# Weight conversion: the exact integer sum of exponent word and sign-and-rounding word is made by GpSimd instead of VectorE

## The chip, the cores and the metric

The kernel runs on one core of one Trainium2 chip. The metric is device time in microseconds; three runs of the kernel before took 594.98, 594.09 and 592.65 us, median 594.09 us. A core has TensorE (matmul), VectorE, ScalarE, GpSimd and SyncE, each with its own queue of instructions; in profiles they are PE (with PEld for weight loads), DVE, ACT, POOL and SP.

## The reference

A recurrent attention block (RWKV6) is followed by a two-layer network with an exact GELU:

```python
# r, k, v, w: (4, 8, 768, 48); u: (8, 48)
for t in range(S):
    kt, vt, rt, wt = (k[:, :, t], v[:, :, t], r[:, :, t], w[:, :, t])
    cur = np.einsum('bhd,bhe->bhde', u[None] * kt, vt)
    y[:, :, t] = np.einsum('bhd,bhde->bhe', rt, state + cur)
    state = wt[:, :, :, None] * state + np.einsum('bhd,bhe->bhde', kt, vt)

# x: y as (3072, 384); w_in: (384, 2048); w_out: (2048, 384), both float64
h = x @ w_in
g = 0.5 * h * (1.0 + erf(h * inv_sqrt2))
return (g @ w_out).astype(np.float32)
```

The two weight matrices come as float64 (a float32 array times a NumPy float64 scalar). The kernel takes them as 64-bit integers and makes float32 of them on the chip.

## The kernel before

The 3072 tokens are cut into eight blocks x of 384. For each block, `attention` (L373) makes the network's input xT, and `mlp` (L920) multiplies it by w_in, applies GELU and multiplies by w_out. While block x is attended to, the network of block x - 1 runs. The order in which instructions are issued is written out by hand: both are generators, and the strings in PLAN (L38) say, letter by letter, which generator does its next step. In block 0 the letters "." and "s" are the two halves of its attention, in block 1 "." is the network of block 0, "s" the attention of block 1 and "f" the beginning of the next block's; "l" loads, "w" makes masks and sums of w_out, "c" converts weights. Every engine works through its own queue in that order, and waits by semaphore for what it needs.

The weights are converted in blocks 0 and 1, in 16 pieces of 128x768 elements: eight of w_in, then eight of w_out. The steps of one piece, and their lines:

- A piece is loaded by SyncE into `raw`, of which there are five buffers (L212). Piece i + 3 is loaded once piece i is converted in program order, and takes over the buffer of piece i - 2.
- `prepare` (L342) runs on ScalarE: f is the high word's magnitude scaled by 2^-112 (L350), e is made of the low word in two steps, rounding it (L351, L352). f and e have two buffers each (HALFWAY), so piece i + 2 writes over those of piece i.
- `finish` (L355) runs on VectorE: f is shifted left by 3 (L363), e gets the sign of the high word (L365), and the result is the integer sum f + e, written into w_in_sb or w_out_sb (L369). The sum has to be exact in 32 bits; on VectorE it appears in the trace as one custom instruction over 128x1536 half-words.

`conversion` (L324) makes these into four steps of the letter "c": prepare the piece after this one, shift, sign, sum.

Around them in the queues of VectorE, ScalarE and TensorE in block 1 stand these lines, which the prediction speaks of: L472, the products of keys and receptances on TensorE, for six distances h; L525, the update of r and k on VectorE after each, and L536 and L485, which copy the products into a_sb under a mask (L533 does so on ScalarE for the last two distances); L514, the same updates as L525 in two single steps, in block 0; L705, transposes of k on TensorE, and L707, ScalarE's copy of them into kx; L731, products of kx and v; L746, the chain of states on VectorE; L772 and L817, the outputs of attention on TensorE, with a fence (L782, L784) between; L1074, the network's first product, with GELU on ScalarE (L1077, L1079); L1168, its second, which takes w_out_sb two rows of 128 per piece; L864, sums of w_out on VectorE. After block 1, L411, L398, L431 and L405 on VectorE begin the attention of block 2, whose first products are L608. GpSimd (iota, memset, an identity, and four copies at L306) has nothing to do after the first 20 us.

```python
            f = cv.tile([128, PIECE], U32, name="f")
            e = cv.tile([128, PIECE], U32, name="e")
            nc.scalar.activation(out=f.bitcast(F32), in_=hi.bitcast(F32), func=AF.Abs, scale=2.0 ** -112)
            nc.scalar.activation(out=e.bitcast(F32), in_=lo, func=AF.Identity, scale=2.0 ** -51, bias=two)
            nc.scalar.activation(out=e.bitcast(I32), in_=e.bitcast(F32), func=AF.Identity, scale=2.0 ** 22, bias=minus)
```

Of the kernel before, what the change touches and what calls it, by code (L numbers as in the profile page):

```python
# [11 lines left out]
U32 = mybir.dt.uint32  # L12
# [5 lines left out]
ALU = mybir.AluOpType  # L18
# [54 lines left out]
def kernel(  # L73
# [25 lines left out]
    nc = tc.nc  # L99
# [224 lines left out]
    def conversion():  # L324

        i = converted[0]
        if i >= len(pieces):
            return
        converted[0] += 1

        prepare(i + HALFWAY)
        yield
        if wide:
            yield from finish(pieces[i][0], raws[i], *halfway[i])
        for _ in weight_in(i + 3):
            pass
# [18 lines left out]
    def finish(dst, raw, f, e):  # L355

        hi = raw.bitcast(U32).rearrange("p (a b) -> p a b", b=2)[:, :, 1]

        nc.vector.tensor_scalar(out=f, in0=f, scalar1=3, scalar2=None, op0=ALU.logical_shift_left)  # L363
        yield
        nc.vector.scalar_tensor_tensor(out=e, in0=hi, scalar=0x80000000, in1=e,  # L365
                                       op0=ALU.bitwise_and, op1=ALU.bitwise_or)
        yield
        f, e = (z.rearrange("p (a c) -> p a c", a=dst.shape[1]) for z in (f, e))
        nc.vector.tensor_tensor(out=dst.bitcast(U32), in0=f, in1=e, op=ALU.add)  # L369

    xT_of = {}

# [955 lines left out]
```

## Time and profile before

| | |
|---|---|
| median of three runs | 594.09 us (592.65 to 594.98) |
| span of the profiled execution, first to last instruction | 591.6 us |
| TensorE busy (matmul) | 573.7 us, 97% |
| VectorE busy | 453.5 us, 77% |
| ScalarE busy | 279.8 us, 47% |
| GpSimd busy | 8.0 us, 1%, 21 instructions |
| granted TensorE clock | 1.00 throughout |

The page gives the profiled execution's span only; the three times beside it are of other executions. How busy each engine is in the stretches of blocks 0 and 1, in us (number of instructions):

```
core 0: us, PE busy (x) PEld busy (x) DVE busy (x) ACT busy (x) POOL busy (x), PEclk, DMA share, GB/s
30.00:45.00 15.00, 11.81 (x480) 10.20 (x483) 12.58 (x42) 9.80 (x20) 0.00 (x0) 1.00 0.59 190
45.00:60.00 15.00, 14.95 (x230) 9.40 (x229) 14.71 (x22) 11.77 (x24) 0.00 (x0) 1.00 0.86 302
60.00:75.00 15.00, 15.00 (x163) 9.10 (x163) 14.90 (x18) 12.84 (x24) 0.00 (x0) 1.00 0.54 168
75.00:90.00 15.00, 15.00 (x218) 9.73 (x211) 12.92 (x17) 12.86 (x22) 0.00 (x0) 1.00 0.76 274
90.00:105.00 15.00, 15.00 (x248) 9.91 (x250) 14.19 (x30) 13.07 (x18) 0.00 (x0) 1.00 0.17 55
105.00:120.00 15.00, 15.00 (x244) 11.85 (x237) 14.59 (x25) 4.49 (x10) 0.00 (x0) 1.00 0.12 37
```

A busy share says how much an engine had to do, not whether anything waited for it. That is read from the chain of work that ended last, from the waits, and from the order of the instructions in time. An instruction's line in the order of time gives its start, its length, the engine, the line, the operation, output and inputs, and in brackets the idle time before it and what ended it.

### The profile page before, as it was taken

The page shows a single profiled execution, that of the slowest core. Times are in us where ns is not written, and L with a number is a line of the kernel's source. Part 1 is how long each engine was busy: PE and PEld are TensorE (multiplying, and loading weights), DVE is VectorE, ACT ScalarE, POOL GpSimd, SP SyncE. Part 2 cuts the span into 40 slices and gives each one's busy share as a digit, 9 for nine tenths or more (in the row PEclk, how much of TensorE's full clock was granted, in tenths as well). Part 3 has the DMA queues.
Part 4 walks back from the last instruction along what each step waited for, and adds up shares of the span by engine and source line. Part 5 has one row for each costly group of instructions (what it writes and reads, how often), then busy time and mean ns, then how long its engine had stood idle before and what let it go on. Part 6 is the DMA issues. An engine that isn't in the chain of part 4 may idle for free.

```text
span 591.6 us, 17422 instructions
## 1 busy us (share of the span) xinstructions
PE 573.7 (97%) x7522; PEld 510.8 (86%) x7536; DVE 453.5 (77%) x871; ACT 279.8 (47%) x648; POOL 8.0 (1%) x21
## 2 busy tenths in 40 slices
PE   5779999999999999999999999999999999999998
PEld 3566666766799999999999999999999999999997
DVE  5989989998969986787859987688859998421432
ACT  2367889223612558046462458145560465435400
POOL 3100000000000000000000000000000000000000
DMA  6658581020142302241032311330025200210000
GB/s 237 197 192 308 163 287 56 32 89 2 29 140 78 108 22 35 76 125 38 1 61 84 122 38 21 93 120 2 2 34 160 72 2 8 35 46 0 1 14 33
DMA packets 51004, 46.80 MB, mean 79 GB/s; under 512 B 31728, under 2 KB 36080, under 8 KB 50928
## 3 DMA queue, kind: packets, MB, share of 16 engines
q1 hardware_dynamic: 50832, 45.62, 25.6%
q8 instruction: 59, 0.97, 0.7%
q14 instruction: 17, 0.14, 0.1%
q10 hardware_dynamic: 96, 0.07, 0.1%
HBM read 36.24 MB, written 4.72 MB: 69 GB/s over the span
## 4 chain that ended last, share of the span: by engine, by line
PE 91%; DVE 3%; DMA 2%; issue 1%; ACT 1%; SPq 0%; DVEq 0%; ACTq 0%
PE o_ps L1088 33%; PE h_ps L949 16%; PE u_ps L949 14%; PE h_ps L1074 11%; PE d L608 4%; PE o_ps L1168 4%; PE d L472 2%; PE y_ps L772 2%; PE y_ps L817 2%; PE kv_ps L731 2%; DVE st L746 1%; DMA rkw<-in_rkw_dram 1%; DMA raw<-in_w_in_dram 1%; ACT a_sb L533 1%; PE d L599 1%
## 5 line engine op out<-in xcount | busy, mean ns | idle before, releaser
L949 PE MATMUL h_ps<-xT,w_in_sb 128*128 128x192 f32 x480 | 95.5, 330 | 0.4 <-DVE o_sb L1185 0.4
L949 PEld LDWEIGHTS h_ps<-xT,w_in_sb 128*128 128x128 f32 x480 | 79.7, 190 | 4.0 <-ACT g L981 1.5
L1074 PE MATMUL h_ps<-xT,w_in_sb 128*128 128x384 f32 x192 | 64.2, 490 | 0.1
L1074 PEld LDWEIGHTS h_ps<-xT,w_in_sb 128*128 128x128 f32 x192 | 35.8, 190 | 24.1 <-ACT xT L824 0.4
L1088 PE MATMUL o_ps<-w_out_sb,g 128*128 128x192 f32 x224 | 39.7, 326 | 0.0
L1088 PEld LDWEIGHTS o_ps<-w_out_sb,g 128*128 128x128 f32 x224 | 37.0, 190 | 0.3
L949 PE MATMUL u_ps<-s,w_in_sb 128*128 128x192 f32 x192 | 35.3, 327 | 0.0
L624 ACT COPY a_sb<-d 32x256 f32<-32x256 f32 (+8 forms) x90 | 32.6, 363 | 4.6 <-PE d L608 3.1
L472 PEld LDWEIGHTS d<-rkw 64*64 64x64 f32 x1152 | 19.5, 138 | 15.6 <-issue 10.0
L949 PEld LDWEIGHTS u_ps<-s,w_in_sb 128*128 128x128 f32 x192 | 31.7, 190 | 0.2
L1088 PE MATMUL o_ps<-w_out_sb,f 128*128 128x192 f32 x176 | 31.6, 329 | 0.0
L1088 PE MATMUL o_ps<-t,g 128*128 128x192 f32 x176 | 31.4, 329 | 0.0
L1088 PE MATMUL o_ps<-w_out_sb,e 128*128 128x192 f32 x176 | 31.4, 329 | 0.0
L1088 PE MATMUL o_ps<-t,e 128*128 128x192 f32 x176 | 31.2, 328 | 0.0
L1088 PE MATMUL o_ps<-t,s 128*128 128x192 f32 x176 | 30.9, 327 | 0.0
L746 DVE SCALAR_TENSOR_TENSOR st<-st,tot_sb,kv_ps 128x48 f32<-128x48 f32 x160 | 29.0, 258 | 1.7 <-PE kv_ps L731 1.6
L472 PE MATMUL d<-rkw 64*64 64x64 f32 (+1 forms) x1152 | 22.1, 225 | 8.1 <-DMA rkw<-in_rkw_dram 4.1
L641 DVE COPY_PREDICATED a_sb<-quarter,d 128x480 f32<-128x480 uint8 (+5 forms) x54 | 23.2, 438 | 8.6 <-PE d L608 7.3
L1088 PEld LDWEIGHTS o_ps<-t,g 128*128 128x128 f32 x176 | 28.7, 190 | 0.4
L1088 PEld LDWEIGHTS o_ps<-w_out_sb,e 128*128 128x128 f32 x176 | 28.7, 190 | 0.3
L1088 PEld LDWEIGHTS o_ps<-w_out_sb,f 128*128 128x128 f32 x176 | 28.7, 190 | 0.3
L1088 PEld LDWEIGHTS o_ps<-t,e 128*128 128x128 f32 x176 | 28.8, 190 | 0.2
(165 smaller groups left out, 1134.0 us busy)
## 6 DMA issues: line engine op xcount, KB each, us to landing
rkw<-in_rkw_dram SPq DMA_DIRECT2D x54, 256.0 KB, 3.8
raw<-in_w_out_dram SPq DMA_DIRECT2D x8, 768.0 KB, 4.4
v_in<-in_v_dram SPq DMA_DIRECT2D x8, 584.0 KB, 3.9
raw<-in_w_in_dram SPq DMA_DIRECT2D x5, 768.0 KB, 7.0
out_dram<-o_sb SPq DMA_DIRECT2D x20, 192.0 KB, 2.0
rkw<-kx SPq DMA_DIRECT2D x72, 48.0 KB, 2.1
rkw<-in_rkw_dram SPq DMA_DIRECT2D x6, 384.0 KB, 5.5
raw<-in_w_in_dram SPq DMA_DIRECT2D x9, 256.0 KB, 5.1
```

The lines of the kernel that those rows point to most:

```text
L472: nc.tensor.matmul(d[half[p], g, n * width:(n + 1) * width], lhsT=kc[half[g], b, i, p], rhs=right(half[g], b, i, p), start=True, stop=True)
L608: nc.tensor.matmul(o[half[p], i * 3 * C // 2:(i + 1) * 3 * C // 2], lhsT=kc[half[g], n // NI, n % NI, p], rhs=rx[half[g], 2 * n + p], star ...
L624: nc.scalar.copy(out=at[z, g, first:behind, (a + 1) * h:], in_=d[z, :, :, to] if g == slice(None) else d[z, :, to])
L641: nc.vector.copy_predicated(out=an[:, :, :, :, (a + 1) * h:], mask=mask.to_broadcast(data.shape), data=data)
L731: nc.tensor.matmul(kv_ps[half[g], p, i * D:(i + 1) * D], lhsT=k_t(b, i, p, g), rhs=vs(b, i, g)[half[p], 0:D], start=True, stop=True)
L746: nc.vector.scalar_tensor_tensor(out=stq[:, q, c], in0=stq[:, q, c - 1] if c else b4[:, q, NC - 1], scalar=totq[:, q, c:c + 1], in1=kvs[q ...
L772: nc.tensor.matmul(y[p][half[g ^ swap(b)], i * C:(i + 1) * C], lhsT=vs(b, i, g)[half[p]], rhs=at[half[p], g, b * NI + i, :], start=(i == 0 ...
L817: nc.tensor.matmul(ys[b][0][c % 2][half[g ^ swap(b)], i * C:(i + 1) * C], lhsT=src[half[g], o:o + G], rhs=rc[half[g], b, i, c % 2], start= ...
L949: nc.tensor.matmul(o, lhsT=lhsT, rhs=rhs, start=start, stop=True, skip_group_check=True)
L1074: nc.tensor.matmul(h_ps, lhsT=w_in_sb[:, f // FI, j, f % FI * 128:(f % FI + 1) * 128], rhs=xT[:, j, :], start=(j == 0), stop=(j == NJ - 1))
L1088: nc.tensor.matmul(o, lhsT=lhs(j), rhs=rhs(j), start=start and j == 0, stop=(j == HF - 1), skip_group_check=True)
L1168: nc.tensor.matmul(o, lhsT=block(i, f // HF, f % HF), rhs=w_out_sb[:, f, :], start=(f == 0), stop=(f == NF - 1))
```

## The change

The sum at L369 is issued on GpSimd's queue. Operands, output and operation are as before; on GpSimd the addition of 32-bit words is an instruction of its own, over 128x768 words. The order of the steps stays, and so do the buffers.

```diff
@@ -366,7 +366,7 @@
                                        op0=ALU.bitwise_and, op1=ALU.bitwise_or)
         yield
         f, e = (z.rearrange("p (a c) -> p a c", a=dst.shape[1]) for z in (f, e))
-        nc.vector.tensor_tensor(out=dst.bitcast(U32), in0=f, in1=e, op=ALU.add)
+        nc.gpsimd.tensor_tensor(out=dst.bitcast(U32), in0=f, in1=e, op=ALU.add)
 
     xT_of = {}
 
```

## The prediction

> **What bounds it now.** I read the chain that ended last first, over the whole span and then from the start to 180 us; then the instructions that touch the tile f; then the two queues around the conversion, in order of time; then what little GpSimd does.
>
> ```profile
> PE 91%; DVE 3%; DMA 2%; issue 1%; ACT 1%; SPq 0%; DVEq 0%; ACTq 0%
> ```
>
> ```profile
> 84.16 1.53 PE d L472 x96
> 85.69 7.94 PE o_ps L1168 x24
> 93.62 1.53 PE d L472 x96
> 95.16 2.78 PE o_ps L1168 x8
> 97.93 1.31 PE kt_ps L705 x12
> 99.24 1.29 PE o_ps L1168 x4
> 100.54 1.54 PE kv_ps L731 x96
> ```
>
> The columns are start, length and work. From 45 us on, the chain is TensorE's own list with no gap. VectorE's time is worth nothing there unless TensorE comes to wait for it; lateness of VectorE, ScalarE or the weights costs as soon as it uses up its slack.
>
> ```profile
> L369 DVE CUSTOM_DVE_ANT_0 w_in_sb<-f,e x8: 941/954/958, 31.8 to 73.1; 128x1536 uint16<-128x1536 uint16 x8
> L369 DVE CUSTOM_DVE_ANT_0 w_out_sb<-f,e x8: 953/958/960, 75.4 to 106.8; 128x1536 uint16<-128x1536 uint16 x8
> ...
>   ACT f L350: 0.6, 1
> ```
>
> These are the sixteen additions, 0.95 us each, 31.8 to 107.8 us. The last line is the only wait that an addition ends: ScalarE, once, 0.6 us, for a buffer of f. TensorE never waited for one.
>
> **The change, part by part.** *Removed:* 16 additions from VectorE's queue. From one start to the next instruction's they hold 0.87 us (97.89 to 98.76), so 14 us in all. Does that shorten anything? On TensorE between 25 and 122 us, waits ended by VectorE are 1.0 (L525), 0.7 (fence) and 0.5 us (L363) on the weight loads, all before 43 us, where only addition 0 has gone before. The gain on the chain is therefore 0, at most about 1 us.
>
> *Added:* 16 additions of 128x768 words on GpSimd. No two-input GpSimd instruction is in this trace. The nearest rows:
>
> ```profile
> L271 POOL MEMSET a_sb<- 128x1536 f32 x1 | 1.4, 1378 | 2.2 <-DVE a_sb L270 2.2
> L301 POOL MEMSET rkw<- 128x512 f32 x1 | 0.5, 525 | 8.4 <-DVE rkw L514 8.4
> ...
> L306 POOL COPY rkw<-ident x4: 403/412/1134, 17.0 to 18.4; 32x128 f32<-32x128 f32 x4
> ```
>
> The two memsets give (1378 - 525) / 1024 = 0.83 ns per element and 0.10 us fixed. One addition reads two words per element: at twice the memset's rate 0.10 + 768 x 1.67 ns = 1.38 us, the lower end. The copy of 128 elements takes 412 ns undisturbed: (412 - 98) / 128 = 2.45 ns per element, so 0.10 + 768 x 2.45 ns = 1.98 us, and 3.86 us if a second input doubles it, the upper end. I take 2.0 us: the copy is the only row that reads and writes, and its scattered writes make up for its missing input.
>
> *The wait it brings.* The same copies show what GpSimd and VectorE do to each other:
>
> ```profile
> 17.30 1.03 DVE L485 COPY_PREDICATED a_sb<-mask,d 128x768 f32<-128x768 uint8 x1
> 18.25 0.95 DVE L525 TENSOR_TENSOR rkw<-rkw,tot_sb 128x768 f32<-128x768 f32 x1
> ```
>
> ```profile
> 18.35 1.13 POOL L306 COPY rkw<-ident 32x128 f32<-32x128 f32 x1
> ```
>
> Three copies beside L485, which has one operand in SBUF (the mask) and one in PSUM, took 0.40 to 0.41 us. The fourth began 0.10 us into L525, which reads two SBUF tensors, and took 1.13 us: it ended at 19.48, 0.28 us after L525. So GpSimd waited for a two-read VectorE instruction. The reverse, VectorE held by GpSimd, isn't shown; I price it at the whole rest of the addition, with 0 as the other end. What stands behind an addition in VectorE's queue is mostly of this kind: L363 (0.55 us for 768 words, against 0.95 us for L365, so at about twice the rate; taken as blocked), L365 and L525 (two reads); only L536, L485 and L746 are free.
>
> The Trainium skill, page "SBUF — State Buffer", section "Who interferes with whom", says that GpSimd shares one port pair with VectorE as an exclusive lock for a whole instruction, against VectorE instructions with two SBUF inputs or in a two-port mode: the loser waits it out. The copy's 1.13 us agrees for GpSimd as loser; by the page VectorE loses as much, and without it the sum below would be 0. The page "GPSIMD Engine Reference", section 3.1, measures a 2048-element addition at 4497 ns there and 2293 ns on VectorE; its estimate for 768 would be 1.69 us, and the sum about +3 us.
>
> *The walk.* I lay the queue out again with 2.0 us per addition, each starting when L365 is done and the port is free, and later instructions kept in program order. An addition with a two-read instruction behind it costs VectorE 2.0 in place of 0.87: +1.1 us. One that lies under COPY_PREDICATED gives back 0.87. L365 of pieces 3 to 12 then stands at +0.2, -0.7, +0.5, +1.6, +1.9, +3.0, +3.2, +2.4, +3.2, +4.3 us; two VectorE waits for ScalarE (0.44 and 1.31 us near 82 us) take up what piece 10 gives back. TensorE's bursts L472 don't notice: L525 ends 3.5 to 6 us ahead of each. At 95 us it is otherwise:
>
> ```profile
> 93.53 0.95 DVE L864 TENSOR_TENSOR t<-w_out_sb 128x768 f32<-128x768 f32 x1
> 95.22 1.76 DVE L525 TENSOR_TENSOR rkw<-rkw,tot_sb 128x1536 f32<-128x1536 f32 x1 [0.74 <-PE d L472]
> 96.90 0.95 DVE L365 SCALAR_TENSOR_TENSOR e<-raw,e 128x768 uint32<-128x768 uint32 x1
> ```
>
> ```profile
> 94.68 0.89 ACT L350 ACTIVATE f<-raw 128x768 f32<-128x768 f32 x1
> ...
> 97.46 1.59 ACT L533 COPY a_sb<-d 32x768 f32<-32x768 f32 x2
> 99.08 1.50 ACT L707 COPY kx<-kt_ps 128x768 f32<-128x768 f32 x2
> ```
>
> L525 ends at 96.98 and the transposes L705 that read its k start at 97.77: slack 0.8 us. The walk has L525 at 99.85 to 101.6 (addition 11 until 94.2, L365 of piece 12, L864, addition 12 until 98.5, L363, L864, L525). L705 is 3.8 us late. On ScalarE, L350 of piece 14 waits for addition 12 because both use one of two buffers of f, and queued behind it are L533 and L707, whose kx the matmuls L731 read; L707 would end at 104.45 instead of 100.58, no later than L731 needs with TensorE 3.8 us late. Next, L365 of piece 15 comes behind L746 and its addition ends at 115.75; TensorE's rows 14 of L1168, at 110.5 before, stand at 114.3: another 1.4 us. The stage after adds 0 to 0.4 us (VectorE's next deadline, L608 at 136.06, has 1.5 us). Together 5.5 us.
>
> That has GpSimd take the port as soon as it falls free. If VectorE's next two-read instruction always takes it first, additions run only in VectorE's gaps: addition 11 begins at 92.1, 12 at 94.1, L525 ends at 99.2 (L705 +1.5), L731 waits for kx (+2.0), and the last addition ends at 113.4 to 116.3, for 2.9 to 5.8 us in all. The trace doesn't say which; I take 4.5 us, between them. The earlier stretch costs nothing: additions 0 and 1, startable at 30.5 and 34.6 us, are wanted first by L350 at 39.1 and 48.7; the L514s behind them may be 1 to 2 us late, against the fence at 41.7 us at most +1.2 (taken as 0, kept for the range). No DMA moves: the raw buffers come free with L365, not with the addition, and GpSimd's queue is empty after 19.5 us.
>
> *Sum:* span 591.6 + 4.5 = 596.1. The three runs lie 1.1 to 3.4 us above that span, their median 2.5: 598.6 us.
>
> **Rivals.** *Hidden (not slower).* VectorE isn't held by a GpSimd read, or the addition is near 1.38 us. For it: the slack at every L472, 2.3 us or more from each addition's end to its weights' first matmul (least for addition 3, 58.8 to 61.1); ScalarE's one wait (for addition 3 behind L525, L536 and L485) goes too. Against: the 1.13 us copy. Two-read and double-rate work on VectorE from 45 to 107 us is L365 14 x 0.87, L363 14 x 0.47, L525 6 x 1.7, L431 2.7 and L864 3 x 0.87, together 34; 62 - 34 leaves 28 us for 14 additions, 2.0 each if all were packed perfectly. Well under that, at 1.4 us, it decides: +0 to 1, 594.1 to 595.
>
> *A slow addition.* At 3.86 us the port needs 34 + 14 x 3.86 = 88 us where 62 are there; about 6 us of slack go off: +20, 614 us. At 2.7 us it would be some +10, 604. It decides from 2.4 us on. Against it: the memset's 0.83 ns.
>
> *Faster.* VectorE's relief would have to remove TensorE waits; the three that it ends come to 2.2 us on the weight loads, so 592 us at best, and 3 us of gain has no place to come from.
>
> **Numbers.** What a measurement here can tell from no change is 0.5%, 3.0 us, so slower is above 597.1 and faster below 591.1. Forecast 0.55, with its own range 596 to 601, of which a fifth lies below 597.1; slow addition 0.14; hidden 0.27; faster 0.04. Slower 0.44 + 0.14 = 0.58, same 0.11 + 0.27 = 0.38, faster 0.04. The range takes in most of hidden and the milder half of slow: 593.8 to 607.
>
> **What would show it.** Right: sixteen GpSimd additions near 2 us (longer where they wait); L363, L365 or L525 longer than 0.55, 0.95 and 1.75 us, or gaps before them; TensorE waiting for L525 at L705, for L707 at L731 and for the last addition at L1168; ScalarE's L350 waiting for GpSimd. Wrong: VectorE's rows unchanged beside GpSimd's reads, additions under 1.5 us, or TensorE without a gap from 95 to 116 us.

## The result, and the profile after

Seventeen runs of each: 598.04 us after (595.07 to 599.67), 593.50 us before (592.24 to 597.27). The ratio is 1.0060, 95% interval 1.0045 to 1.0075: 3.6 us slower, between 2.7 and 4.5. (The two medians alone are 4.5 us apart, at the upper end of that interval; the ratio is made from all the runs.) The forecast was 598.6 us in a range of 593.8 to 607, with 0.58 on "slower by over 0.5%". The profiled execution's span is 597.5 us, against 591.6.

The groups of instructions that touch f, kernel after: count, then shortest, median and longest in ns, then when the first and the last began; under them, who waited for these.

```profile
L363 DVE TENSOR_SCALAR f<-f x16: 544/556/2174, 27.7 to 106.5; 128x768 uint32<-128x768 uint32 x16
L369 POOL TENSOR_TENSOR w_in_sb<-f,e x8: 1804/2314/3332, 30.1 to 77.3; 128x768 uint32<-128x768 uint32 x8
L369 POOL TENSOR_TENSOR w_out_sb<-f,e x8: 1818/2277/3268, 80.3 to 113.1; 128x768 uint32<-128x768 uint32 x8
...
  ACT f L350: 1.5, 3
  PEld kt_ps L705: 1.0, 1
```

ScalarE waits three times for a buffer of f, 1.5 us in all. The last line is a weight load of TensorE at 33 us, in block 0. L705 reads no sum there: it reads k, and the L514 that updates k stood 2.17 us instead of 0.55 beside addition 0 (30.77 to 32.94 us), so that TensorE's matmuls of L705 began only at 33.09, after a wait of 0.56 us.

An addition takes 1.80 us on GpSimd when nothing disturbs it (0.95 on VectorE), and up to 3.3 us when something does. What does is seen in the order of time, kernel after, VectorE first:

```profile
63.06 1.76 DVE L525 TENSOR_TENSOR rkw<-rkw,tot_sb 128x1536 f32<-128x1536 f32 x1
64.74 2.17 DVE L363 TENSOR_SCALAR f<-f 128x768 uint32<-128x768 uint32 x1
66.83 1.87 DVE L536 COPY_PREDICATED a_sb<-mask,d 128x768 f32<-128x768 uint8 x1
```

```profile
63.17 3.32 POOL L369 TENSOR_TENSOR w_in_sb<-f,e 128x768 uint32<-128x768 uint32 x1 [3.57 <-DVE e L365]
```

The addition is released at 63.17, 0.11 us into L525, and ends at 66.49: it waited until L525's end at 64.82 and then needed 1.67 us. L363, next in VectorE's queue, begins at 64.74 on paper and ends at 66.91: 2.17 us where 0.55 is its length, so it stood for 1.62 us. So the two exclude each other, and here the one that waits gets the next turn. A whole hold like this one costs VectorE 1.62 us, and the removed addition gives back 0.87.

What TensorE made of it, kernel after, between 97 and 113 us:

```profile
97.34 1.60 PE L472 MATMUL d<-rkw 64*64 64x32 f32 x96
98.87 2.85 PE L1168 MATMUL o_ps<-w_out_sb,g 128*128 128x384 f32 x8
101.90 1.53 PE L705 MATMUL kt_ps<-ident,rkw 128*128 128x128 f32 x12 [0.18 <-DVE rkw L525]
103.27 1.46 PE L1168 MATMUL o_ps<-w_out_sb,g 128*128 128x384 f32 x4
104.65 1.61 PE L731 MATMUL kv_ps<-v_in,kx 64*64 64x48 f32 x96
106.20 2.85 PE L1168 MATMUL o_ps<-w_out_sb,g 128*128 128x384 f32 x8
108.97 0.93 PE L772 MATMUL y_ps<-a_sb,v_in 64*64 64x64 f32 x48
111.93 0.93 PE L772 MATMUL y_ps<-a_sb,v_in 64*64 64x64 f32 x48 [2.03 <-DVE st L746]
```

In the kernel before this stretch had no gap. Its end there, with the chain of states L746 on VectorE first:

```profile
102.31 3.58 DVE L746 SCALAR_TENSOR_TENSOR st<-st,tot_sb,kv_ps 128x48 f32<-128x48 f32 x20
```

```profile
100.47 1.61 PE L731 MATMUL kv_ps<-v_in,kx 64*64 64x48 f32 x96
102.01 2.85 PE L1168 MATMUL o_ps<-w_out_sb,g 128*128 128x384 f32 x8
104.79 1.82 PE L772 MATMUL y_ps<-a_sb,v_in 64*64 64x64 f32 x96
106.54 6.72 PE L1168 MATMUL o_ps<-w_out_sb,g 128*128 128x384 f32 x20
```

In the kernel after, TensorE waits 0.2 us for L525 at L705 and 2.03 us for L746 in the middle of L772: its second half writes a pair of PSUM banks that L746 still reads (three such pairs take turns in the kernel, and the second y_ps gets the pair of the first kv_ps). And the whole stretch is late already when it begins: L472 starts at 97.34, not at 93.55. That 3.8 us arose before 53.5 us, where L1074's first long run starts (49.67 before). So the profile has two places, and the experiments had to price them apart.

### The profile page after: what moved, and what is told of

It is laid out like the page before. It is cut to its first block, busy times and chain, and to the rows that moved or that the text cites. A ratio compares the mean times of both kernels' runs of the same rounds, so it can differ in the third digit from the quotient of the medians.

```text
span 597.5 us, 17440 instructions
## 1 busy us (share of the span) xinstructions
PE 577.2 (97%) x7536; PEld 512.0 (86%) x7536; DVE 456.8 (76%) x855; ACT 280.0 (47%) x648; POOL 46.2 (8%) x37
## 5 line engine op out<-in xcount | busy, mean ns | idle before, releaser
L1074 PE MATMUL h_ps<-xT,w_in_sb 128*128 128x384 f32 x192 | 64.4, 491 | 2.9 <-DMA xT<-ysb 2.0
L1074 PEld LDWEIGHTS h_ps<-xT,w_in_sb 128*128 128x128 f32 x192 | 35.7, 190 | 27.4 <-issue 3.9
L472 PEld LDWEIGHTS d<-rkw 64*64 64x64 f32 x1152 | 19.6, 138 | 14.8 <-issue 10.6
L746 DVE SCALAR_TENSOR_TENSOR st<-st,tot_sb,kv_ps 128x48 f32<-128x48 f32 x160 | 29.0, 257 | 1.7 <-PE kv_ps L731 1.6
L1088 PEld LDWEIGHTS o_ps<-t,s 128*128 128x128 f32 x176 | 28.8, 190 | 0.1
```

The source lines that it names most:

```text
L472: nc.tensor.matmul(d[half[p], g, n * width:(n + 1) * width], lhsT=kc[half[g], b, i, p], rhs=right(half[g], b, i, p), start=True, stop=True)
L746: nc.vector.scalar_tensor_tensor(out=stq[:, q, c], in0=stq[:, q, c - 1] if c else b4[:, q, NC - 1], scalar=totq[:, q, c:c + 1], in1=kvs[q ...
L1074: nc.tensor.matmul(h_ps, lhsT=w_in_sb[:, f // FI, j, f % FI * 128:(f % FI + 1) * 128], rhs=xT[:, j, :], start=(j == 0), stop=(j == NJ - 1))
L1088: nc.tensor.matmul(o, lhsT=lhs(j), rhs=rhs(j), start=start and j == 0, stop=(j == HF - 1), skip_group_check=True)
```

## The experiments

Each was timed in five rounds against the kernel before on the same chip. A kernel that chooses the engine by piece has one more line, so its numbers behind L369 are one higher (L746 is L747 there).

**The changed kernel again.**

> The changed kernel once more, for a second profile of it. Two theories of its 4.5 us. Port: VectorE's two-read and double-rate instructions are held while GpSimd's additions read, the lateness grows from 50 us on, and TensorE pays from 98 to 113 us (L705, L772, L1168). Early: additions 0 and 1 hold L514, TensorE stands still near 38 us, the clock falls, the transfers of xT land late, and TensorE's first long run of L1074 begins late; what follows is covered by that. Port expects that run's start to vary between the profiles (49.7 us in the kernel before, 53.5 in the first profile of this one) while L1168's last rows stay 4 to 6 us late; early expects the run to begin 3 to 4 us late again. Both: 4 to 5 us above the kernel before.

596.82 us against 593.53; ratio 1.0061 (1.0040 to 1.0082). L1074's long run began at 52.74 us, L1168's last rows at 112.05 (106.54 before). The two late waits came back (0.16 us at L705, 2.03 at L772). The run was 3.1 us late again, as "early" had expected, but not all of that comes from additions. ScalarE's L350 of piece 1 waits for that piece's weights to land; it began at 29.02 us, against 27.70 before, and the granted clock was 0.50 between 30 and 32 us, while the first addition began at 32.60. From L350 of piece 1 to the long run it was 21.97 us in the kernel before, 26.78 in the first profile of the change, 23.72 in this one. So this profile alone doesn't decide between the two theories.

**Which additions cost.** The edit, with another set of pieces each time:

```diff
-        nc.gpsimd.tensor_tensor(out=dst.bitcast(U32), in0=f, in1=e, op=ALU.add)
+        engine = nc.gpsimd if converted[0] <= 2 else nc.vector
+        engine.tensor_tensor(out=dst.bitcast(U32), in0=f, in1=e, op=ALU.add)
```

> Only the additions of pieces 0 and 1 are on GpSimd, the other fourteen on VectorE as before. Early: 2.5 to 4 us slower than before, with TensorE idle for 2 us near 38 us and a granted clock under 0.8 after it. Port: L514 is held for 1 to 2 us, but VectorE's lateness is taken up before 50 us; 0 to 1 us slower.

> Additions 0 and 1 are on VectorE as before, the other fourteen on GpSimd. Port: 3 to 5 us slower than before, with TensorE waiting at L705 or L772 between 98 and 112 us. Early: at most 2.5 us slower, since the first stall is gone and with it most of the cost.

> Only the eight additions of w_out (pieces 8 to 15) are on GpSimd. Port: VectorE has 6 us of slack up to piece 10 and 0.8 us at L525 before L705; five additions before it are on GpSimd at some 0.9 us of lateness each, less the waits of 0.4, 1.3 and 0.7 us that VectorE has there: 2 to 4 us slower than before. Early: no more than 1 us slower.

| additions on GpSimd | ratio (95%) | us over 593.53 | L350 of piece 1 to the long run | wait at L772 |
|---|---|---|---|---|
| 0 and 1 | 1.0022 (1.0001 to 1.0043) | +1.3 | 22.41 us | none |
| 2 to 15 | 1.0061 (1.0037 to 1.0085) | +3.6 | 22.13 us | 2.03 us |
| 8 to 15 | 1.0044 (1.0025 to 1.0063) | +2.6 | 22.17 us | 2.02 us |
| all (again) | 1.0061 (1.0040 to 1.0082) | +3.6 | 23.72 us | 2.03 us |

(Microseconds are the ratio less one, times 593.53.) The early theory falls as the main cause: without additions 0 and 1 the cost is all there, and alone they cost 1.3 us with 0.1 to 2.6 in the interval, more than the 0 to 1 of "port" and less than the 2.5 to 4 of "early". The two parts, 1.3 and 3.6, sum to 4.9 where all sixteen cost 3.6; the intervals (2.4 to 4.9 for all, 2.2 to 5.0 for 2 to 15) allow it, so the share of additions 0 and 1 is known only roughly. "Port" holds in part. It priced 8 to 15 rightly, but said that lateness grows from 50 us on, and then 2 to 7 should add to it. The wait at L772 is the same 2.0 us with and without them. So the next pair asked where VectorE's lateness begins to count.

> Additions 2 to 9 are on GpSimd, the other eight on VectorE. Catching up: VectorE's lateness from these is gone when it waits for TensorE at L525 after the product of distance 16 (near 86 us), so TensorE has no new wait at L705 or L772: within 1 us of the kernel before. Running total: the lateness grows from 50 us on and reaches L705: 2 us or more slower.

> Only additions 13 and 14 are on GpSimd. Catching up: they hold L365 of piece 14 and L363 of piece 15 for 1.6 us each and save 0.87 us each, so L746 is 1.5 us late; TensorE's second half of L772 needs the bank that L746 reads and has 0.1 to 0.2 us of slack, so a wait of 1.3 us at L772 and none at L705; 1 to 2 us slower. Weights: if the last additions' own lateness were what counts, no wait at L772 and less than 0.5 us.

Additions 2 to 9: 593.37 us against 593.58, ratio 0.9998 (0.9979 to 1.0016), nothing. Their holds are there (an addition takes 2.7 us in the mean for w_in, L363 0.82 us instead of 0.55), yet TensorE has no wait at L705 or L772. VectorE's queue in that run shows why:

```profile
80.67 1.81 DVE L363 TENSOR_SCALAR f<-f 128x768 uint32<-128x768 uint32 x1 [0.51 <-ACT f L350]
82.53 0.96 DVE L365 SCALAR_TENSOR_TENSOR e<-raw,e 128x768 uint32<-128x768 uint32 x1
...
84.72 1.76 DVE L526 TENSOR_TENSOR rkw<-rkw,tot_sb 128x1536 f32<-128x1536 f32 x1 [0.23 <-PE d L473]
```

The same place in the kernel before:

```profile
83.58 0.96 DVE L365 SCALAR_TENSOR_TENSOR e<-raw,e 128x768 uint32<-128x768 uint32 x1 [1.31 <-ACT e L352]
...
85.75 1.76 DVE L525 TENSOR_TENSOR rkw<-rkw,tot_sb 128x1536 f32<-128x1536 f32 x1 [0.23 <-PE d L472]
```

L363 is held for 1.26 us. That goes into the 1.31 us that VectorE used to wait for ScalarE before L365, and then VectorE waits for TensorE, 0.23 us as in the kernel before. The product of distance 16 (L472, L473 here) and the L525 behind it are 1.67 us apart in both kernels (84.08 to 85.75 before, 87.87 to 89.54 after): whatever was late on VectorE has been caught up there.

Additions 13 and 14 alone: 594.66 us, ratio 1.0019 (1.0001 to 1.0037), 1.1 us. VectorE and then TensorE:

```profile
99.11 2.57 DVE L365 SCALAR_TENSOR_TENSOR e<-raw,e 128x768 uint32<-128x768 uint32 x1
101.61 0.95 DVE L865 TENSOR_TENSOR t<-w_out_sb 128x768 f32<-128x768 f32 x1
102.48 2.18 DVE L363 TENSOR_SCALAR f<-f 128x768 uint32<-128x768 uint32 x1
104.58 3.57 DVE L747 SCALAR_TENSOR_TENSOR st<-st,tot_sb,kv_ps 128x48 f32<-128x48 f32 x20
```

```profile
101.34 1.61 PE L732 MATMUL kv_ps<-v_in,kx 64*64 64x48 f32 x96
102.88 2.85 PE L1169 MATMUL o_ps<-w_out_sb,g 128*128 128x384 f32 x8
105.66 0.93 PE L773 MATMUL y_ps<-a_sb,v_in 64*64 64x64 f32 x48
107.95 0.93 PE L773 MATMUL y_ps<-a_sb,v_in 64*64 64x64 f32 x48 [1.36 <-DVE st L747]
```

Two holds of 1.6 us, less two additions of 0.87: the chain of states begins 3.24 us after L731's first matmul, against 1.84 us before (100.47 to 102.31), so 1.40 us late, and TensorE waits 1.36 us. With all of 10 to 14 on GpSimd it begins 3.90 us after (104.65 to 108.55), 2.06 us late, and TensorE waits 2.03 us. The slack at this place is under 0.05 us. "Weights" is out: nothing waits for a sum itself in this profile. Additions 10 to 12 were not run alone.

**Is it the reading?** Both kernels keep every sum on VectorE and give GpSimd something beside it that nobody uses:

```diff
+        beside = s_home[:, 0:PIECE].bitcast(U32)
+        nc.vector.memset(beside[:, 0:1], 0)
+        nc.gpsimd.tensor_tensor(out=beside, in0=beside, in1=beside, op=ALU.add)   # beside_read
+        for _ in range(2):                                                        # beside_write
+            nc.gpsimd.memset(beside, 0)
         nc.vector.tensor_tensor(out=dst.bitcast(U32), in0=f, in1=e, op=ALU.add)
```

(One or the other; s_home is cleared once at its making.)

> The kernel before, with every sum on VectorE; beside each, GpSimd adds 128x768 words of a scratch tile to themselves into the same tile (released by a one-word VectorE memset after L365), and nothing reads it. Port: VectorE's two-read and double-rate instructions are held for up to 1.7 us beside each, sixteen times, with nothing saved for it: L369 or L363 or L525 stretched, 4 to 12 us slower. Rival (the cost comes from the sum's result or the buffers being late, for ScalarE and TensorE): within 1 us of the kernel before.

> As the run beside_read, but GpSimd only writes the scratch tile: two memsets of 128x768 words, 0.74 us each, in the place of its addition. If the hold is by GpSimd's reading: L365, L369 and L525 keep 0.95, 0.95 and 1.75 us, at most L363 is longer, 0 to 1.5 us slower. If any GpSimd instruction on this memory holds VectorE: 3 to 10 us slower, and L525 or L369 stretched by 0.7 us and more.

The reading neighbour: 608.12 us, ratio 1.0232 (1.0207 to 1.0258), 13.8 us slower, more than the theory's 4 to 12. The writing one: 593.94 us, 0.9998 (0.9983 to 1.0014), nothing. VectorE's groups between 25 and 125 us, first beside reads, then beside writes (L364 and L366 are L363 and L365; L529 and L530 are L525):

```profile
L364 DVE TENSOR_SCALAR f<-f 128x768 uint32<-128x768 uint32 x16 | 18.0, 1123 | 0.0
L529 DVE TENSOR_TENSOR rkw<-rkw,tot_sb 128x1536 f32<-128x1536 f32 x5 | 12.6, 2512 | 0.0
```

```profile
L366 DVE SCALAR_TENSOR_TENSOR e<-raw,e 128x768 uint32<-128x768 uint32 x16 | 15.3, 954 | 0.0
L364 DVE TENSOR_SCALAR f<-f 128x768 uint32<-128x768 uint32 x16 | 12.2, 761 | 0.0
L530 DVE TENSOR_TENSOR rkw<-rkw,tot_sb 128x1536 f32<-128x1536 f32 x5 | 8.8, 1752 | 0.3 <-PE d L477 0.2
```

Beside reads, L525 lasts 2.51 us in the mean instead of 1.75, and TensorE waits 5.9 us for it at L705, the longest of several waits. Nobody waits for GpSimd's result there, so the time starts from the holds; TensorE's granted clock, which was 0.50 from 106 to 112 us in that profile, adds to it. Beside writes the two-read instructions keep their lengths (the sum itself, which runs beside the memsets, 0.953 to 0.957 us, L525 1.752) and only the double-rate L363 is held, at 89.36 us for example 1.20 us instead of 0.55, behind one memset; TensorE's wait at L772 is 0.5 us in that profile, too little for its times to show.

The Trainium skill, page "SBUF — State Buffer", section "Who interferes with whom", says just this: an exclusive lock, held for the instruction, in which a VectorE instruction with two SBUF inputs meets only a GpSimd instruction that reads SBUF, and one in a two-port mode meets any. The runs agree: the two-read L525 is held beside reads (2.51 us in the mean) and not beside writes (1.752). That L363 is in a two-port mode is taken from its rate, 0.55 us against 0.95 for L365; no run shows the mode.

## Why the prediction was right

- *No gain on the chain.* Right. With additions 2 to 9 off VectorE the ratio is 0.9998.
- *The addition at 2.0 us.* 1.80 to 1.84 us undisturbed. The bounds of 1.38 and 3.86 held it. An estimate by proportion from the 4497 ns for 2048 elements of the Trainium skill, page "GPSIMD Engine Reference", section 3.1, gave 1.69: 0.11 us too little.
- *VectorE held by GpSimd.* Right, and so for L363, taken as blocked without a row that showed it. (Of the three unhindered copies the first ran mostly beside an L536, from 16.98 us, not beside L485; both are COPY_PREDICATED.) The order of turns, left open between two walks, is the first walk's. A hold behind an addition costs 1.62 - 0.87 = 0.75 us, not 1.1.
- *The running lateness ("L365 of pieces 3 to 12 then stands at +0.2, ... +4.3 us", "L705 is 3.8 us late").* This step failed. Additions 2 to 9 cost nothing; the lateness starts anew at the L525 of distance 16, because VectorE waits for TensorE there. The trace before has that wait (0.23 us at 85.75); the walk doesn't name it and carried lateness over it. L705 waits 0.2 us.
- *What is late next.* The walk went from L705 to the last addition at L1168 (1.4 us). No profile shows a wait for a sum there: in the first profile of the change the last addition ends at 115.49 us, and its rows, twelve matmuls after 112.79, begin near 116.8. Nor does L731 wait for L707. In between it passed L746, which it listed only as free of holds; it isn't held, but stands behind L363 and L365 that are, and TensorE needs its banks less than 0.05 us after it lets go of them. That is the 2.0 us at L772.
- *The earlier stretch, "at most +1.2 (taken as 0, kept for the range)".* 1.3 us, 0.1 to 2.6.
- *"GpSimd's queue is empty after 19.5 us."* Not any more: its memset and copies L301 and L306 stand behind additions 0 and 1 and moved from 16.4 to 36.9 us, at no cost that shows.

In sum 4.5 us were forecast and 3.6 measured. The mechanism was right: GpSimd's reads hold VectorE, and TensorE pays between 97 and 113 us. That the size came out is in part luck. The 3.8 us charged at L705 and the 1.4 at L1168 were 0.2 and nothing; in their place stand 2.0 at L772, some 1.3 before 53 us, which the sum took as 0, and the falls of the granted clock told of below, for which it had no term.

## What to carry to other kernels

Two engines that share a memory port make one queue: moving work from VectorE to GpSimd frees VectorE only while VectorE runs instructions that don't need the port, and the neighbour's hold takes the place of the one removed (here 1.62 us for 0.87). Lateness on a side engine isn't a running total, as additions 2 to 9 show: begin again at each point where that engine waits for the critical one, and add up only from the last such point to the next deadline. List every deadline behind it, PSUM banks still being read among them; an instruction that can't be held itself is late with those in front of it.

## What was not expected

A wait of 2.0 us is not all that TensorE loses. After the same wait at L772, the twenty matmuls of L1168 took 6.72 us in both profiles of the change, but 8.41 with additions 2 to 15 and 7.87 with 8 to 15. Those two show the granted clock fall, here with 2 to 15 (columns: stretch, length, busy time of five engines, granted clock, transfers):

```profile
106.00:108.00 2.00, 0.47 (x30) 0.50 (x33) 2.00 (x11) 0.00 (x0) 0.00 (x0) 1.00 0.00 0
108.00:110.00 2.00, 2.00 (x35) 1.29 (x27) 2.00 (x5) 0.00 (x0) 1.31 (x1) 0.68 0.03 8
110.00:112.00 2.00, 2.00 (x4) 1.01 (x3) 2.00 (x2) 0.00 (x0) 1.08 (x1) 0.50 0.00 0
```

In the first profile of the change it fell to 0.50 between 40 and 42 us, after a gap of 2.14 us from 37 us on (1.10 in the kernel before). This, and transfers of xT that then landed up to 5.4 us after their issue (3.5 before), lie in the 3.8 us by which that execution was late at 53 us. The Trainium skill, page "TensorE: Matmul & The Clock Gate", Part 1, has the clock fall to half after an idle window of some 3.4 us; here two of four gaps of 2.0 us were enough, and two were not. What decides it, and how much of the 1.3 us of additions 0 and 1 is this, stays open.

The timed executions give a hint of what these falls cost. The mean granted clock was under 1.000 in 19 of 33 executions of the kernel before, and in 10 of 12 with additions 2 to 15. Where it was 1.000, the kernel before took 593.5 us in the mean (14 executions) and the one with 2 to 15 took 595.1 and 595.7: 1.9 us apart, about the waits at L772 and L705 alone, instead of 3.6. Two executions are few, and a low mean doesn't say where the clock fell: in the first profile of the change it was also 0.50 between 10 and 12 us, before any addition.

No version beats the kernel before: TensorE's list sets its time from 45 us on, and the placement that costs nothing (2 to 9) gains nothing.
